# Banded attention and a routed two-layer network: weights in longer runs with strided columns, one batch fewer transposed on chip, narrower appends, products on zeros, and a new order of work

## The chip, the cores and the metric

The kernel runs on one core of one Trainium2 chip. The core has a matrix engine (TensorE, "PE" in the profile, with "PEld" for its loads of the stationary operand), VectorE ("DVE"), ScalarE ("ACT"), GpSimd ("POOL") and SyncE ("SP"), each with its own queue of instructions in a fixed order, and 16 DMA engines that all queues feed. The metric is device microseconds for one execution, lower is better.

## The reference

Attention over a band of 32 positions to either side, 8 batches, 8 heads, 576 positions, 64 columns a head:

```python
scores = scale * np.matmul(q, k.transpose(0, 1, 3, 2))
mask = np.abs(pos[:, None] - pos[None, :]) <= window      # window = 32
scores = np.where(mask, scores, -1000000000.0)
attn = np.exp(scores - np.max(scores, axis=-1, keepdims=True))
attn = attn / (np.sum(attn, axis=-1, keepdims=True) + 1e-09)
out = np.matmul(attn, v)
```

Its output, as 4608 tokens of 512 columns, goes through a network with 8 experts. Each token uses the one with the largest logit:

```python
logits = x @ w_gate + modality_bias[modality_id]          # modality_id is 0 or 1
e_idx = np.argmax(logits, axis=1)
gate_w = softmax(logits)[np.arange(N), e_idx]
for e in range(E):
    h = np.maximum(x[mask] @ w1[e], 0.0)                  # 512 -> 1024
    out[mask] = gate_w[mask, None] * (h @ w2[e])          # 1024 -> 512
```

## The kernel before

The bias decides the expert nearly alone, so the kernel computes, for each of the two modalities, only the expert with the largest bias, and checks at the end that every token chose that expert. If not (or if a count is too large), a branch runs a slow general version. With the inputs used here it isn't taken.

The program is one long list of named steps, `ORDER`, written out by hand. A loop reads it and calls one small function for each name. Every engine executes its own share of the list in this order and waits where its data aren't ready; nothing is moved afterwards. A step's numbers are its indices, `/a` or `/v` names the engine (ScalarE or VectorE), and the digits behind a colon are the PSUM banks it uses, of eight.

For each batch b (0 to 7), with the heads in two groups g of four:

- `l b.u.g` (L215, GpSimd's DMA queue) loads queries (u = 0) or keys (u = 1) of a group into one of eight `qkin` buffers, converted to bf16. `t b.g.u` (L582, VectorE) transposes them in 32x32 blocks into `qk`.
- `MA`, `MB` (L591, L595) write the band's mask into PSUM by a product with the identity `ident`; `SA`, `SB` (L614) add the scores; batches 0 and 1 use the former, later batches are masked by `M` (L639, VectorE) after the exponential. `sa`, `sb` (L622, L625, ScalarE) are the exponentials into `pt`.
- The values come in one of two ways. `lv` (L220) loads a half straight into `vt` in runs of 64 columns. `lw` (L226) loads it in long runs into a `qkin` buffer; then `tv` (L237, VectorE) transposes it, `TV` (L250, TensorE) multiplies it with columns of the identity, 20 products, and `vc` (L264 ScalarE or L266 VectorE) copies the result into `vt`. Batches 0 to 3 go the second way.
- `V` (L658, TensorE) multiplies with the values for a pair of heads, `v` (L668, L669, VectorE) normalises into `xt`.
- `H b.m` (L678, TensorE, four products) takes 128 tokens of `xt` as weights and multiplies them with a one-hot matrix `oh` (`o`, L576) that sorts the tokens: those of modality 0 to the left, those of modality 1 to the right. `a` (L695, ScalarE) appends both parts to `xl`, each in a window of W columns, whose place is read from a register (`Ko` loads the registers). Windows overlap, and the later one writes over the unused end of the earlier one. `J` and `j` (L708, L716) do the same for the token numbers in `cl`.

For each of 18 groups t of 256 sorted tokens, and one of 128 in the middle (t = 18):

- `U t.mp` (L819, TensorE, eight products) is the first layer with `w_sb` (W1 of the modality) as weights; `u` (L834 ScalarE, L832 VectorE) applies the maximum with 0. `D t.s.half` (L842, four products) is the second layer, `y` (L854, L856) scales it, and `O` (L862, GpSimd) writes 128 rows to their places with an indirect DMA.
- `G` (L746, L749) and `r`, `E` compute the router's logits, the check and the row numbers for two groups at a time. `W which.i` (L792, GpSimd's DMA queue) loads the weights of layer `which`.

The constants are `K...` steps: `Km`, `Ki` load the bias and the modality ids (SyncE's queue), `Kd` (L473, VectorE) converts the ids into `midr`, `Kt`, `Kr` count the tokens in front of each, `Kn` and `Ka` build masks on GpSimd, `Kf0` is a part of the check of counts on GpSimd. `Z0` to `Z6` gather the check: `Z2` (L886, L889, GpSimd), `Z3` (L892 to L896, VectorE), `Z4` (L900, TensorE), `Z5` (L902, VectorE) make the word `t_i`. All engines load it (L1038) and branch on it (L1040).

## Time and profile before

| | us |
|---|---|
| median of 3 runs (lowest, highest) | 228.79 (228.74, 230.57) |
| the profiled execution | 228.53 |
| its span in the trace | 226.9 |
| TensorE busy | 202.0 (89%) |
| VectorE busy | 158.1 (70%) |
| ScalarE busy | 143.9 (63%) |
| GpSimd busy | 103.2 (45%) |

The span runs from the first to the last instruction of the program; the rest of an execution's time lies around it. TensorE's products are pipelined: one starts before the one ahead of it ends, so the distance between starts is the cost in a dense stretch, and a group's busy time divided by its count is near it, but for the last product's own time. The mean duration of one, also printed, is longer. A line of the timeline reads: start, length, engine, line of the code, operation, output<-inputs, shape, count, and in brackets the idle time of the engine ahead of it and what ended it. A line of the chain reads: start, length, what ran.

### The profile page before, as it was taken

The numbers are of one execution on the slowest core, as the hardware profiler recorded it, in microseconds if no ns is written. First come the engines' busy times: TensorE is split into PE (matmuls) and PEld (weight loads), VectorE is DVE, ScalarE is ACT, GpSimd is POOL, SyncE is SP. The second block draws the span as 40 slices with busy tenths as digits, with TensorE's granted clock in tenths as the row PEclk, the third lists the DMA queues.
The fourth block names the chain that finished last, engine by engine and source line by source line (L and its number), as shares of the span: only waits on it lengthen the run. The fifth ranks groups of instructions, "written<-read, shape, count | busy, mean of one in ns | idle before, by whom it ended". The sixth has DMA issues, their size and how long they took to land.

```text
span 226.9 us, 6569 instructions
## 1 busy us (share of the span) xinstructions
PE 202.0 (89%) x2693; PEld 146.3 (64%) x2720; DVE 158.1 (70%) x312; ACT 143.9 (63%) x219; POOL 103.2 (45%) x211
## 2 busy tenths in 40 slices
PE   0498887899999999999999999999999999999940
PEld 0257566689768666777667776775875777666510
DVE  1588999989998999699889892976528036334210
ACT  8179789999889789689577876732654332103420
POOL 6988443951502878148408014400450402436670
PEclk9999999999999999999999999999999999999995
DMA  4999999999999948979989111900140299214441
GB/s 74 155 196 203 202 192 212 207 188 175 207 210 191 123 100 153 183 133 174 181 97 133 60 49 63 128 5 0 51 185 3 50 174 194 95 46 188 185 141 60
DMA packets 32774, 30.44 MB, mean 134 GB/s; under 512 B 20664, under 2 KB 23776, under 8 KB 32736
## 3 DMA queue, kind: packets, MB, share of 16 engines
q0 software_dynamic: 32512, 29.90, 73.9%
q8 instruction: 23, 0.38, 0.7%
q14 instruction: 15, 0.12, 0.2%
q1 hardware_dynamic: 224, 0.05, 0.2%
HBM read 40.96 MB, written 9.70 MB: 223 GB/s over the span
## 4 chain that ended last, share of the span: by engine, by line
PE 79%; DVE 6%; ACT 6%; issue 3%; DMA 2%; SPq 1%; POOL 1%; DVEq 0%; POOLq 0%; ACTq 0%
PE banks L842 28%; PE banks L819 28%; PE banks L658 6%; PE banks L614 5%; PE banks L250 4%; PE banks L678 4%; ACT pt L622 3%; DVE qk L582 2%; ACT xl L695 2%; PE banks L746 2%; DMA mid<-in_moe_modality_id_dram 2%; DVE xt L669 1%; PE banks L708 1%; ACT pt L625 1%; SPq L283 1%
## 5 line engine op out<-in xcount | busy, mean ns | idle before, releaser
L819 PE MATMUL banks<-xl,w_sb 128*128 128x256 bf16 x576 | 71.1, 273 | 0.2 <-ACT xl L695 0.2
L842 PE MATMUL banks<-w_sb,hT 128*128 128x512 bf16 x261 | 66.6, 379 | 1.6 <-issue 0.3
L862 POOL DMA_INDIRECT out_dram<-ys,ix x37 | 39.6, 1070 | 53.7 <-issue 29.7
L819 PEld LDWEIGHTS <-w_sb 128*128 128x128 bf16 x576 | 54.3, 98 | 11.0 <-issue 0.6
L622 ACT ACTIVATE pt<-banks 128x1536 bf16<-128x1536 f32 x32 | 46.4, 1453 | 16.0 <-PE banks L614 15.6
L842 PEld LDWEIGHTS <-hT 128*128 128x128 bf16 x296 | 27.0, 98 | 25.3 <-issue 0.8
L582 DVE STREAM_TRANSPOSE qk<-qkin 128x576 int32<-128x576 int32 x32 | 38.3, 1239 | 0.5 <-DMA qkin<-in_k_dram 0.5
L834 ACT ACTIVATE hT<-banks 128x512 bf16<-128x512 f32 x41 | 24.0, 595 | 19.0 <-PE banks L819 18.9
L695 ACT CAST xl<-banks 128x768 f32 x40 | 32.2, 805 | 5.7 <-PE banks L678 3.5
L639 DVE TENSOR_TENSOR pt<-pt,mask 128x1920 bf16<-128x1920 bf16 x24 | 27.3, 1146 | 4.7 <-ACT pt L625 4.2
L856 DVE TENSOR_SCALAR ys<-banks,gw 128x512 f32<-128x512 f32 x20 | 14.8, 743 | 20.4 <-PE banks L842 14.1
L832 DVE TENSOR_SCALAR hT<-banks 128x512 bf16<-128x512 f32 x33 | 22.4, 684 | 8.1 <-PE banks L819 7.9
L669 DVE TENSOR_TENSOR xt<-banks,recs 128x640 bf16<-128x640 f32 x32 | 26.4, 825 | 1.1
L854 ACT ACTIVATE ys<-banks,gw 128x512 f32<-128x512 f32 x17 | 11.5, 686 | 19.1 <-PE banks L842 17.0
L658 PE MATMUL banks<-vt,pt 128*128 128x65 bf16 x576 | 22.6, 193 | 1.2 <-ACT pt L625 0.9
L658 PEld LDWEIGHTS <-pt 128*128 128x128 bf16 x576 | 20.9, 97 | 4.0 <-issue 1.6
L614 PE MATMUL banks<-qk 32*128 32x192 bf16 (+1 forms) x640 | 19.5, 245 | 1.6 <-DVE xt L669 0.5
L614 PEld LDWEIGHTS <-qk 32*128 32x128 bf16 x640 | 12.9, 95 | 8.9 <-issue 6.8
L781 POOL CAST ix<-ixf 128x4 int32<-128x4 f32 (+1 forms) x10 | 2.8, 279 | 32.2 <-DVE ixf L778 32.2
L716 ACT CAST cl<-banks 4x192 f32 x40 | 12.3, 307 | 5.7 <-PE banks L708 5.0
L678 PE MATMUL banks<-oh,xt 128*128 128x128 bf16 x160 | 14.1, 219 | 0.8 <-ACT pt L622 0.7
L678 PEld LDWEIGHTS <-xt 128*128 128x128 bf16 x160 | 10.9, 98 | 3.5 <-issue 0.7
(165 smaller groups left out, 202.5 us busy)
## 6 DMA issues: line engine op xcount, KB each, us to landing
qkin<-in_k_dram POOLq DMA_DIRECT2D x16, 288.0 KB, 8.1
qkin<-in_q_dram POOLq DMA_DIRECT2D x16, 288.0 KB, 7.8
w_sb<-in_moe_w_dram POOLq DMA_DIRECT2D x4, 1024.0 KB, 11.8
qkin<-in_v_dram POOLq DMA_DIRECT2D x8, 288.0 KB, 7.2
vt<-in_v_dram POOLq DMA_DIRECT2D x8, 288.0 KB, 6.6
pt<-in_moe_w_dram POOLq DMA_DIRECT2D x2, 1024.0 KB, 11.5
out_dram<-ys,ix POOLq DMA_INDIRECT x37, 2.8
mid<-in_moe_modality_id_dram SPq DMA_DIRECT2D x3, 8.0 KB
```

Of the source, the lines that this page charges most:

```text
L582: nc.vector.transpose(qk_t[b % 2][:, g, at:at + S].rearrange("p (t r) -> p r t", r=R), Ct["l", b, u, g][:].bitcast(I32).rearrange("p (r j) ...
L614: nc.tensor.matmul(st[:, h, WIN * i_:WIN * i_ + w_], qk[32 * h:32 * h + 32, c_, QK + k0:QK + k0 + P], qk[32 * h:32 * h + 32, c_, q0:q0 + w ...
L622: nc.scalar.activation(pt[:, :, 2 * part:2 * part + 2, 0:WIN], st[:, :, 0:2 * WIN].rearrange("p h (j c) -> p h j c", c=WIN), ACT.Exp, scal ...
L639: by[eng or "v"].tensor_tensor(out=p_ap, in0=p_ap, in1=mask[:], op=ALU.mult)
L658: nc.tensor.matmul(o_ap, pt[:, c1:c1 + P], vt[:, g0 + j, 0:D + 1], start=(m == 0 and i_ == 0), stop=(i_ == len(mine) - 1), skip_group_chec ...
L669: nc.vector.tensor_tensor(out=x_t[b % NX][:, hp].rearrange("p m (h d) -> p h m d", h=2), in0=o_v[:, :, :, 0:D], in1=rec.unsqueeze(3).to_br ...
L678: nc.tensor.matmul(ph[:, kd, :], x_t[b % NX][:, kd, m, :], Ct["o", b][:, m, :], start=(kd == 0), stop=True, skip_group_check=True)
L695: ins = nc.scalar.copy(windows(xl, n_kd, P, NM * b + m), src)
L819: ins = nc.tensor.matmul(ph[:, u_, :], w1[:, kd, P * mi:P * mi + P], xl[:, kd, c0:c0 + n_], start=(kd == 0), stop=(kd == n_kd - 1))
L834: nc.scalar.activation(o_ap, i_ap, ACT.Relu)
L842: nc.tensor.matmul(Ct["D", t_, s_], Ct["h", t_][:, kf, P * s_:P * s_ + P], w2[:, kf, :], start=(kf == 0), stop=(kf == n_kf - 1))
L862: ins = nc.gpsimd.indirect_dma_start(out=out, out_offset=bass.IndirectOffsetOnAxis(ap=ix[:, k_, n_:n_ + 1], axis=0), in_=Ct["y", t_, s_][: ...
```

## The change

Seven things change.

1. The weights of the first layer are split by `(ki ko)` instead of `(ko ki)`: partition ki holds four neighbouring rows of W1, one run of 16 KB in DRAM, instead of four runs of 4 KB. Its products then need the inputs' columns ki*4 + kd on partition ki. So `xt` becomes tokens by 512 columns, and `H` takes every fourth column as weights. The gate's weights are split the same way.
2. The second layer's weights are split so that a partition holds pairs of neighbouring rows, runs of 4 KB instead of 2 KB. The order of the 1024 hidden columns changes with it, and `U` takes every second column of W1 as weights.
3. Batch 3's values are loaded with `lv`. Only batches 0, 1 and 2 use `lw`, `tv`, `TV`, `vc`.
4. The append windows are 88 columns wide instead of 96, and the limits of the check follow.
5. A new step `X` multiplies a matrix of zeros with itself, twice, 512 columns each; its output isn't read. It stands eight times in the list.
6. The list has a new order throughout.
7. The slow version follows the new layouts.

```diff
-Kh l0.1.0 Ki Km Kv1/v Kv3/v Ke Kw Kd l0.0.0 Kn0 Kc1 l0.0.1 Kj Kc0 l0.1.1 lw0.0 lw0.1 Kt0:2 Kv0/v t0.0.1 Kn1 MA0.0:4567
...
-y16.0/a O18.0 O16.1 O17.1 O17.0 O16.0
+Km l0.1.1 Kh Kw t0.1.1 l0.0.1 Kv1/v t0.1.0 Ke Ki Kj lw0.0 l0.1.0 Kn0 Kn1 Kq0/a Kq1/a Kp0/a X7:2 X1:3 X4:7 l0.0.0 Kv0/v
...
+y16.1/a O16.1 Z2 Z3 Z4:3 Z5
...
-    W = 96
+    W = 88
...
-    x_t = [const.tile([P, n_kd, NM, P], BF16, name=f"xt{i}") for i in range(NX)]
+    x_t = [const.tile([P, NM, HD], BF16, name=f"xt{i}") for i in range(NX)]
...
-        nc.gpsimd.dma_start(wg_sb[:], moe_w_gate.rearrange("(ko ki) e -> ki ko e", ki=P))
+        nc.gpsimd.dma_start(wg_sb[:], moe_w_gate.rearrange("(ki ko) e -> ki ko e", ki=P))
...
-            gs.memset(lv_[:, 1], 48.0 * 48.0)
-            gs.memset(lv_[:, 1, :, 1:NM - 1], 32.0 * 32.0)
+            gs.memset(lv_[:, 1], (W - 48.0) ** 2)
+            gs.memset(lv_[:, 1, :, 1:NM - 1], (W - 64.0) ** 2)
...
-            out=x_t[b % NX][:, hp].rearrange("p m (h d) -> p h m d", h=2),
+            out=x_t[b % NX][:, :, P * hp:P * hp + P].rearrange("p m (h d) -> p h m d", h=2),
...
-            nc.tensor.matmul(ph[:, kd, :], x_t[b % NX][:, kd, m, :], Ct["o", b][:, m, :],
+            nc.tensor.matmul(ph[:, kd, :], x_t[b % NX][:, m, kd::n_kd], Ct["o", b][:, m, :],
...
-    W1P, W2P = "a (ko ki) f -> ki (a ko) f", "a (ko ki) d -> ki (a ko) d"
+    W1P, W2P = "a (ki ko) f -> ki (a ko) f", "a (c ki e) d -> ki (a c) (e d)"
...
-                ins = nc.tensor.matmul(ph[:, u_, :], w1[:, kd, P * mi:P * mi + P], xl[:, kd, c0:c0 + n_],
+                ins = nc.tensor.matmul(ph[:, u_, :], w1[:, kd, 2 * P * (mi // 2) + mi % 2:2 * P * (mi // 2 + 1):2], xl[:, kd, c0:c0 + n_],
...
+    def X(_, i):
+        for h in range(2):
+            nc.tensor.matmul(bank([P, 512]), zero_b[:, 0:P], zero_b[:], start=True, stop=True, skip_group_check=True)
```

What the new order does shows best at two places. The first is VectorE at the start. `mid` holds the modality ids, `qk<-qkin` is a transpose, `c` the ids as flags. Before:

```order
L288 MEMSET mid_103 40x256
L232 MEMSET xl 128x64 x4
L430 MEMSET e_119 128x1 x8
L301 MEMSET zero_b 128x256
L302 MEMSET one_f 128x1
L473 CAST midr<-mid_103 40x128
L232 MEMSET xl 128x64 x2
L582 STREAM_TRANSPOSE qk_77<-qkin_69 128x18x32
L494 TENSOR_SCALAR c_125<-banks 128x40
L582 STREAM_TRANSPOSE qk_77<-qkin_70 128x18x32
```

After:

```order
L288 MEMSET mid_103 40x256
L301 MEMSET zero_b 128x256
L302 MEMSET one_f 128x1
L582 STREAM_TRANSPOSE qk_77<-qkin_69 128x18x32
L232 MEMSET xl 128x64 x2
L582 STREAM_TRANSPOSE qk_77<-qkin_70 128x18x32
L430 MEMSET e_119 128x1 x8
L232 MEMSET xl 128x64 x2
L473 CAST midr<-mid_103 40x128
```

The conversion of the ids, which waits for their load, stood ahead of the first transpose and now stands behind the second.

The second place is GpSimd's queue at the end. `out_dram<-ys` is a write of 128 rows, `nm<-ne` and `re` are parts of the check (Z2), `fl<-rm` too (Z6), `t_i` is the word that decides the branch. Before:

```order
L862 DMA out_dram<-ys_97,ix 4608x512
L862 DMA out_dram<-ys_95,ix 4608x512
L862 DMA out_dram<-ys_98,ix 4608x512
L862 DMA out_dram<-ys_96,ix 4608x512
L862 DMA out_dram<-ys_93,ix 4608x512
L1038 TENSOR_LOAD t_i
L1040 COMPARE_AND_BRANCH
```

After:

```order
L862 DMA out_dram<-ys_97,ix 4608x512
L874 TENSOR_SCALAR fl<-rm 128x1
L875 TENSOR_SCALAR fl<-rm 128x1
L862 DMA out_dram<-ys_98,ix 4608x512
L862 DMA out_dram<-ys_93,ix 4608x512
L886 TENSOR_SCALAR re<-ixf 128x40
L889 TENSOR_TENSOR nm<-ne,re 128x320
L1044 TENSOR_LOAD t_i
L1046 COMPARE_AND_BRANCH
```

The two operations of Z2, which stood among the row writes of the last groups, now stand behind the last write, ahead of the load of `t_i`. Their followers on VectorE and TensorE (Z3, Z4, Z5) move with them. In the new file the lines behind L907 are six higher.

102 lines of the change are left out of this document (52 added, 50 removed).

## The prediction

> **What bounds the kernel now.** I read the shares of the page's chain of work, then a table of busy time by stage, then the start in order of time, then the end.
>
> ```profile
> PE 79%; DVE 6%; ACT 6%; issue 3%; DMA 2%; SPq 1%; POOL 1%; DVEq 0%; POOLq 0%; ACTq 0%
> ```
>
> ```profile
> core 0: us, PE busy (x) PEld busy (x) DVE busy (x) ACT busy (x) POOL busy (x), PEclk, DMA share, GB/s
> 8.40:20.00 11.60, 10.14 (x139) 6.49 (x140) 10.57 (x24) 6.99 (x7) 9.77 (x38) 1.00 1.06 190
> 20.00:30.00 10.00, 8.89 (x190) 6.32 (x187) 9.39 (x14) 8.09 (x10) 6.14 (x18) 1.00 1.10 194
> 30.00:42.50 12.50, 9.49 (x213) 8.54 (x214) 12.03 (x16) 11.94 (x15) 6.48 (x13) 1.00 1.15 207
> 60.00:100.00 40.00, 39.63 (x589) 28.82 (x593) 36.36 (x62) 33.44 (x53) 18.55 (x53) 1.00 1.09 166
> 218.40:226.90 8.50, 0.00 (x0) 0.00 (x0) 0.15 (x1) 0.58 (x1) 2.16 (x3) 0.73 0.32 109
> ```
>
> TensorE carries 79% of the chain. From about 50 us on it has no gap worth naming (39.63 of 40 us in the fifth row), so there only removed TensorE work counts. Before 42.5 us it is not the bound: VectorE is (12.03 of 12.50, 9.39 of 10.00), with ScalarE close behind. After 218.4 no engine computes much: 8.5 us of rows written out, a branch and the closing of the program. So there are three accounts: the start, TensorE's work, the end.
>
> The start, from the chain (first row) and the timelines of VectorE, TensorE and ScalarE:
>
> ```profile
> 4.19 3.67 DMA mid<-in_moe_modality_id_dram
> ...
> 7.98 0.32 DVE L473 CAST midr<-mid 40x128 bf16<-40x128 int32 x1 [5.99 <-DMA mid<-in_moe_modality_id_dram]
> 8.27 1.20 DVE L582 STREAM_TRANSPOSE qk<-qkin 128x576 int32<-128x576 int32 x1
> ...
> 10.64 0.83 PE L614 MATMUL banks<-qk 32*128 32x192 bf16 x16 [0.40 <-DVE n1s L497]
> 11.40 1.46 PE L591 MATMUL banks<-neg,ident 128*128 128x384 bf16 x4
> 14.20 0.82 PE L591 MATMUL banks<-neg,ident 128*128 128x384 bf16 x4
> 42.49 1.03 PE L819 MATMUL banks<-xl,w_sb 128*128 128x256 bf16 x8 [0.17 <-ACT xl L695]
> ...
> 11.52 1.45 ACT L622 ACTIVATE pt<-banks 128x1536 bf16<-128x1536 f32 x1 [4.82 <-PE banks L614]
> 14.31 1.45 ACT L622 ACTIVATE pt<-banks 128x1536 bf16<-128x1536 f32 x1 [1.34 <-PE banks L614]
> 28.56 1.45 ACT L622 ACTIVATE pt<-banks 128x1536 bf16<-128x1536 f32 x1 [1.71 <-PE banks L614]
> 32.28 2.24 ACT L264 CAST vt<-banks 128x1152 bf16<-128x1152 f32 x2 [0.43 <-PE banks L250]
> 34.41 4.16 ACT L695 CAST xl<-banks 128x768 f32 x5
> ...
> L237 DVE STREAM_TRANSPOSE xl<-qkin 128x576 int32<-128x576 int32 x8 | 9.3, 1241 | 0.0
> L669 DVE TENSOR_TENSOR xt<-banks,recs 128x640 bf16<-128x640 f32 x32 | 26.4, 825 | 1.1
> L668 DVE RECIPROCAL recs<-banks 128x10 f32<-128x10 f32 x32 | 6.8, 213 | 5.4 <-PE banks L658 5.4
> ```
>
> VectorE stands idle for 5.99 us behind a wait for the modality ids, although the first query and key loads are in SBUF before that:
>
> ```profile
> L215 POOL DMA_DIRECT2D qkin<-in_k_dram x1: 722/722/722, 1.5 to 1.5; - x1
> ...
> DMA to landing us min/median/max: 4.5/4.5/4.5
> ...
> L215 POOL DMA_DIRECT2D qkin<-in_q_dram x1: 592/592/592, 2.2 to 2.2; - x1
> ...
> DMA to landing us min/median/max: 5.2/5.2/5.2
> ...
> w_sb<-in_moe_w_dram POOLq DMA_DIRECT2D x4, 1024.0 KB, 11.8
> ```
>
> These are the first key load (issued at 1.5 us, so landed at 6.0), the first query load (issued at 2.2, landed at 7.4), and the weights.
>
> **The change, part by part.**
>
> *New order at the start.* The id cast moves behind the first two transposes. The first starts at 6.0, the second at 7.4, and the first scores at about 8.6 instead of 10.64. First exponential: 9.5 instead of 11.52, a lead of 2.0 us. Between there and the first append (34.41) ScalarE spends 22.9 us in before, 3.5 of them in the three waits quoted (1.34, 1.71, 0.43). The work is the same eight exponential groups, four value copies and the mask copies. The after order has one register load (the append offsets, an estimate of 1.4 us, since it stood inside the 1.71 wait) in the open, so without waits the first append would start near 9.5 + 22.9 - 3.5 + 1.4 = 30.3. VectorE does not allow that: counting its queue from the second transpose on, at 1.1 to 1.2 us a transpose (9.3 / 8) and 1.0 us a reciprocal with its normalisation (33.2 / 32), its eleventh q/k transpose and fourth value transpose end near 29.7. The products of that last half follow (1.2, half of the 2.4 us that a pair of halves takes below) and its copy (1.1, half of the row at 32.28), so the first append starts near 32.0, 2.4 us earlier. From there to the first up-projection stand five appends and five small ones, one exponential and a router group. My count gives 38.9; I allow 0.6 for small waits that a count leaves out and take 39.5 against 42.49. TensorE has then done about the same work (eight masked banks' worth, five value halves, eight attention outputs in both; within 0.4 us). Term: -3.0 us. Bounds: -1.5 (half lost to waits) and -4.5 (the count holds and the waits of 42 to 51 us go too).
>
> The weights must be there. From the first landing at 6.0, sixteen more loads of 0.295 MB stand ahead of the first weight of 1.05 MB; at the 0.20 MB/us of the window rows that is 1.45 us a load, so W1.1 lands near 6.0 + 16 x 1.45 + 5 = 34 to 36, W1.0 near 40, W2.1 near 47. The U groups want them at 39.5, 43 and 52. GpSimd must issue in time: the new order puts the small operations of the overflow check (Kf0) ahead of W1.1; by a count of its queue the issue still comes some 8 us ahead of that landing, while earlier loads are under way.
>
> *Eight product pairs on zeros.* They stand ahead of everything on TensorE, which has nothing to do until 8.5 us; one pair (0.4 us) stands in a wait before 26 us. Zero cost. What they may bring is that the four mask products take 0.82 (row at 14.20) and not 1.46 us (row at 11.40), though PEclk says 1.00 for both. [...]
>
> *Batch 3's values by strided load.* Two of eight halves lose their transposes, products and copies.
>
> ```profile
> 30.95 2.41 PE L250 MATMUL banks<-ident,xl 128*128 128x64 bf16 x40 [0.96 <-DVE xl L237]
> ```
>
> A pair of halves, 40 products, lasts 2.2 us (2.41 less the drain of the last one, 0.2). One pair goes, from the stage where TensorE is dense: -2.2 us. VectorE loses 2.5 us and ScalarE or VectorE 2.2, both hidden under TensorE. The two loads that come instead land before 69 us by the same queue count; the products on them stand near 67 and 74 us, the first needing only the first load (63 us): zero, with 4 us to spare.
>
> *Strided weights.* H loads every fourth column of xt, U every second of w_sb, at the same number of instructions.
>
> ```profile
> L250 PEld LDWEIGHTS <-xl x160: 97/125/125, 18.2 to 66.3; 128*128 128x128 bf16 x160
> L678 PEld LDWEIGHTS <-xt x160: 95/98/125, 33.1 to 173.4; 128*128 128x128 bf16 x160
> 33.64 0.72 PE L658 MATMUL banks<-vt,pt 128*128 128x65 bf16 x18
> 33.16 0.64 PE L678 MATMUL banks<-oh,xt 128*128 128x128 bf16 x8
> 80.18 0.87 PE banks L819 x8
> ```
>
> The L250 products already take every second column as weights. They follow at 56 ns (2.2 us / 40), while the L658 products, one column wider, follow at 31 ns (0.55 / 18, again without the last drain). Either the strided load takes 56 ns, or the output does, which L250 also writes to every second column. A load not held up lasts 97 ns on L250 and 95 on L678, so I put it down to the output, and the load at no more than before. U has 109 ns a product (0.87 / 8): hidden in either case. H has 56 ns (0.45 / 8). Lower end: 0. Upper end: the 56 ns are the load's and step four doubles it to 112, so 160 x 56 ns = +9.0 us. I take 0, by the 97 and 95.
>
> [...]
>
> *Appends of 88 columns.* 704 instead of 768 elements on ScalarE, 40 times; ScalarE is not on the path after 50 us. Zero. The token counts of this draw need at most 76, so the slow branch stays untaken.
>
> *Longer runs of the weights.* Same bytes, 128 and 512 runs instead of 512 and 1024. At most 1 us sooner for each of the second weights, which wait for nobody: zero.
>
> *The end.* Z2 to Z5, the check that decides the branch, stood among the last groups; now they stand behind the very last row write.
>
> ```profile
> 216.80 1.46 PE L842 MATMUL banks<-w_sb,hT 128*128 128x512 bf16 x6
> 220.19 0.97 POOL L862 DMA_INDIRECT out_dram<-ys,ix  x1 [0.30 <-issue]
> L1040 PEldq COMPARE_BRANCH  x1: 4382/4382/4382, 219.2 to 219.2; - x1
> L1040 POOLq COMPARE_BRANCH  x1: 58/58/58, 219.7 to 219.7; - x1
> L1040 POOLq EVENT_SEMAPHORE  x5: 17/43/992, 223.1 to 224.4; - x5
> L889 POOL TENSOR_TENSOR nm<-ne,re 128x320 f32<-128x320 f32 x1 | 0.7, 740 | 2.9 <-DVE ne L783 2.9
> L892 DVE TENSOR_REDUCE fl<-nm 128x1 f32<-128x320 f32 x1 | 0.5, 476 | 0.0
> ```
>
> In before the last product ends at 218.3; the branch is taken by 219.7; TensorE and GpSimd go on only at 223.6 and 223.1, 3.4 to 4.4 us later; the program ends 8.6 us after the product. In after, the last write is issued 1.6 to 2.5 us after the last product, GpSimd's two check operations end at 3.7, VectorE's three at 4.6, the product, the compare and the register loads at about 5.7. If going on again takes 3.4 us as before, and GpSimd's closing 2.5 us (224.4 to 226.9), the end comes 11.7 us after the product: +3.1. If it only takes 1.5 to 2 us because no row writes move any more, +1.4. I take +2.2; nothing hides it, and the fewer writes at the end (one behind the last product instead of two) are in it.
>
> **The sum.** -3.0 - 2.2 + 2.2 = -3.0 us. The profiled execution took 228.53 us (span 226.9), 0.26 under the median 228.79 of the runs shown: 225.5 against its own time, 225.8 against the median. I say 225.6.
>
> **The rivals.**
>
> *The gain at the start does not come.* If GpSimd's small operations or the DMA queue delay W1.1 to 42 us, the first up-projection starts when it did. For: DMA share is 1.06 to 1.15 in the three early rows, so a late issue is not made up. Against: the count leaves 3.5 us. Then -2.2 + 2.2: 228.6, no change.
>
> *The end costs little.* If the branch goes on at once and the check hides under the last write's landing, the sum is -5.2: 223.4; with the start at its bound, 221.9.
>
> *The strided load is slow (the other side).* One place, H's 160 products: at 112 ns, +9.0 us, 234.6. It decides from 75 ns on: 160 x 19 ns eats the 3.0 us. For: L250's 56 ns. Against: 97 against 95 ns.
>
> *The dense stage opens gaps.* The new order could make TensorE wait for ScalarE or VectorE (33.44 and 36.36 of 40 us busy); each has 2 us or more less to do, so I fold this into the first rival.
>
> **How the numbers follow.** A measurement of this kernel can tell about 1%, 2.3 us, from no change. Forecast (224.5 to 227): 0.45. End cheap or start better (221 to 224.5): 0.25. Start lost (227 to 229.5): 0.20. Slow load (above 229.5): 0.10. Faster by over 1% (under 226.5) gets the second case and most of the first: 0.64; within 1%: 0.28; slower: 0.08, since the slow load at partial price ends within 1%. The range 221.0 to 229.0 leaves out the slow load and a little at both ends. The likeliest case's own range is 224.5 to 227.
>
> **What would show it.** Right: first transpose near 6 us, first L819-group near 39.5, 120 L250 products, H at 56 ns a product, a branch about 6 us after the last product, and a close about 11 us after it. Wrong: L819's first group near 42, weights landing after 40, H at 75 ns or more, gaps in TensorE between 60 and 200 us, or an end shorter than 9 us after the last product.

## The result and the profile after

The kernel after the change takes 230.38 us, the median of 20 runs (229.77 to 231.33). The kernel before, run beside it, takes 228.76 us (20 runs, 227.98 to 230.94). The ratio is 1.0053, with a 95% interval of 1.003 to 1.0077: half a per cent slower, less than the 1% that the forecast counted as a change. The forecast was 225.6 us with a range of 221.0 to 229.0, so the result lies outside the range and on the other side. The profiled execution took 229.87 us, and its span is 228.2 us. The ratios of the experiments leave out runs that lie over 1.5% above the fastest of their kernel; where that drops most runs, the range of all is given first.

The three accounts of the forecast, read from both traces:

| | before | after | measured | forecast |
|---|---|---|---|---|
| span's start to the first up-projection | 42.49 | 41.38 | -1.11 | -3.0 |
| first up-projection to the end of the last product | 175.76 | 173.27 | -2.49 | -2.2 |
| end of the last product to the close | 8.68 | 13.51 | +4.83 | +2.2 |
| span | 226.93 | 228.16 | +1.23 | -3.0 |

The gain in the dense part came near the forecast. The start gave a third of what was expected, and the end took back more than twice what was expected.

The shares of the chain of work, of after:

```profile
PE 78%; POOL 10%; DMA 4%; issue 3%; ACT 1%; DVE 1%; POOLq 0%; ACTq 0%; DVEq 0%
```

GpSimd has 10% of the chain; before it had 1%. The table of busy time by stage, of after (columns as in the prediction's table):

```profile
8.50:20.00 11.50, 8.82 (x176) 6.76 (x177) 9.00 (x26) 8.77 (x8) 9.32 (x36) 1.00 1.02 181
20.00:30.00 10.00, 9.03 (x173) 6.30 (x170) 9.07 (x15) 7.80 (x10) 8.74 (x53) 1.00 1.05 183
30.00:41.40 11.40, 9.58 (x182) 8.63 (x182) 9.46 (x12) 8.52 (x14) 10.19 (x19) 0.85 1.06 215
60.00:100.00 40.00, 40.00 (x597) 29.25 (x595) 36.17 (x61) 31.53 (x48) 19.59 (x23) 1.00 0.99 146
214.70:228.20 13.50, 0.16 (x1) 0.08 (x1) 0.95 (x4) 0.69 (x1) 4.72 (x8) 0.67 0.19 66
```

Between 60 and 100 us TensorE has no gap at all, so the new order does not starve it. Between 30 and 41.4 us no engine but GpSimd is near full (10.19 of 11.40), and the granted clock is 0.85. After the last product GpSimd has 4.72 us of work, where before it had 2.16.

The start, from the timelines of VectorE, TensorE and ScalarE, of after:

```profile
5.78 1.25 DVE L582 STREAM_TRANSPOSE qk<-qkin 128x576 int32<-128x576 int32 x1 [4.19 <-DMA qkin<-in_k_dram]
8.50 0.52 PE L614 MATMUL banks<-qk 32*128 32x192 bf16 x16
9.07 1.45 ACT L622 ACTIVATE pt<-banks 128x1536 bf16<-128x1536 f32 x1 [2.35 <-PE banks L614]
30.18 1.26 DVE L237 STREAM_TRANSPOSE xl<-qkin 128x576 int32<-128x576 int32 x1 [0.93 <-DMA qkin<-in_v_dram]
31.49 2.31 PE L250 MATMUL banks<-ident,xl 128*128 128x64 bf16 x20 [0.86 <-DVE xl L237]
33.84 1.12 ACT L264 CAST vt<-banks 128x1152 bf16<-128x1152 f32 x1 [2.30 <-PE banks L250]
34.86 0.75 ACT L695 CAST xl<-banks 128x704 f32 x1
36.00 0.29 ACT L716 CAST cl<-banks 4x176 f32 x1 [0.39 <-POOL cl L421]
41.38 1.03 PE L819 MATMUL banks<-xl,w_sb 128*128 128x256 bf16 x8
```

The first transpose, scores and exponential stand where the forecast had them (6.0, 8.6 and 9.5 us). Then the lead melts. The value half that the first append waits for is transposed at 30.18, after a wait of 0.93 for its load. Its 20 products take 2.31 us, at half clock, as the window of 3.5 us shows (0.52, third column from the right). Behind the first append (34.86) the first `j0` step waits for GpSimd, which is zeroing `cl`. That zeroing as a row of GpSimd's groups:

```profile
31.50:35.00 3.50, 3.50 (x42) 3.50 (x42) 2.09 (x2) 1.20 (x3) 3.50 (x2) 0.52 1.01 212
...
L421 POOL MEMSET cl<- 128x4736 bf16 x1 | 4.1, 4068 | 0.0
```

It runs from 31.90 to 35.97. A bracket of 0.39 us looks harmless, but it is only the idle time left over: ScalarE reached the step late, and it would have had to wait however early it came.

The end, from the timelines of GpSimd, TensorE and VectorE and from TensorE's sequencer, of after:

```profile
208.53 0.98 POOL L862 DMA_INDIRECT out_dram<-ys,ix  x1 [7.92 <-ACT ys L854]
214.27 0.38 PE L842 MATMUL banks<-w_sb,hT 128*128 128x512 bf16 x1
215.12 0.98 POOL L862 DMA_INDIRECT out_dram<-ys,ix  x1 [0.28 <-POOL ix L781]
216.18 0.26 POOL L874 TENSOR_SCALAR fl<-rm 128x1 f32<-128x1 f32 x1
216.99 1.06 POOL L862 DMA_INDIRECT out_dram<-ys,ix  x1 [0.27 <-issue]
218.36 0.98 POOL L862 DMA_INDIRECT out_dram<-ys,ix  x1 [0.30 <-issue]
219.82 0.74 POOL L889 TENSOR_TENSOR nm<-ne,re 128x320 f32<-128x320 f32 x1
220.60 0.48 DVE L892 TENSOR_REDUCE fl<-nm 128x1 f32<-128x320 f32 x1 [10.15 <-POOL nm L889]
221.80 0.15 DVE L902 TENSOR_SCALAR t_i<-banks 1x1 int32<-1x1 f32 x1 [0.33 <-PE banks L900]
...
L1046 PEldq COMPARE_BRANCH  x1: 4476/4476/4476, 222.6 to 222.6; - x1
```

The last product ends at 214.65. GpSimd still has row writes to issue, with the two small operations of Z6 among them; the last one goes out at 218.36, 3.71 us after the product (1.94 before). Only then come Z2, Z3, Z4 and Z5, the word `t_i` at 221.8, and TensorE's branch, which takes 4.48 us. Each step hands over to the next within 0.3 us, but for the 0.6 us between the word and TensorE's branch, in which the word is loaded: this is one chain on GpSimd and behind it, 13.5 us long.

### The profile page after: what moved, and what is told of

Its sections match the earlier page's. It is cut to its first block, busy times and chain, and to the rows that moved or that the text cites. A ratio compares the mean times of both kernels' runs of the same rounds, so it can differ in the third digit from the quotient of the medians.

```text
span 228.2 us, 6542 instructions
## 1 busy us (share of the span) xinstructions
PE 207.5 (91%) x2696; PEld 146.9 (64%) x2696; DVE 152.6 (67%) x303; ACT 142.7 (63%) x224; POOL 103.1 (45%) x211
## 4 chain that ended last, share of the span: by engine, by line
PE 78%; POOL 10%; DMA 4%; issue 3%; ACT 1%; DVE 1%; POOLq 0%; ACTq 0%; DVEq 0%
PE banks L819 29%; PE banks L842 28%; PE banks L658 7%; PE banks L614 5%; PE banks L678 4%; DMA qkin<-in_v_dram 4%; POOL qkin L215 3%; PE banks L250 2%; POOL out_dram L862 2%; PE banks L746 2%; PE banks L708 1%; ACT xl L695 1%; POOL qkin L226 1%; DVE xl L237 1%; ACT vt L264 0%
## 5 line engine op out<-in xcount | busy, mean ns | idle before, releaser
L842 PE MATMUL banks<-w_sb,hT 128*128 128x512 bf16 x288 | 71.1, 379 | 0.0
L834 ACT ACTIVATE hT<-banks 128x512 bf16<-128x512 f32 x45 | 25.7, 595 | 23.3 <-PE banks L819 23.0
L695 ACT CAST xl<-banks 128x704 f32 x40 | 30.1, 752 | 6.0 <-PE banks L678 5.4
L832 DVE TENSOR_SCALAR hT<-banks 128x512 bf16<-128x512 f32 x29 | 19.7, 684 | 15.9 <-PE banks L819 15.6
L854 ACT ACTIVATE ys<-banks,gw 128x512 f32<-128x512 f32 x20 | 13.5, 688 | 15.9 <-PE banks L842 9.2
L856 DVE TENSOR_SCALAR ys<-banks,gw 128x512 f32<-128x512 f32 x17 | 12.6, 744 | 10.9 <-issue 6.2
L614 PE MATMUL banks<-qk 32*128 32x192 bf16 (+1 forms) x640 | 18.6, 239 | 0.2
L614 PEld LDWEIGHTS <-qk 32*128 32x128 bf16 x640 | 12.1, 93 | 8.3 <-issue 6.0
L678 PEld LDWEIGHTS <-xt 128*128 128x128 bf16 x160 | 11.8, 115 | 4.2 <-issue 0.8
L716 ACT CAST cl<-banks 4x176 f32 x40 | 11.8, 295 | 4.2 <-PE banks L708 2.0
```

Source lines behind the costliest of these rows:

```text
L614: nc.tensor.matmul(st[:, h, WIN * i_:WIN * i_ + w_], qk[32 * h:32 * h + 32, c_, QK + k0:QK + k0 + P], qk[32 * h:32 * h + 32, c_, q0:q0 + w ...
L678: nc.tensor.matmul(ph[:, kd, :], x_t[b % NX][:, m, kd::n_kd], Ct["o", b][:, m, :], start=(kd == 0), stop=True, skip_group_check=True)
L695: ins = nc.scalar.copy(windows(xl, n_kd, P, NM * b + m), src)
L834: nc.scalar.activation(o_ap, i_ap, ACT.Relu)
L842: nc.tensor.matmul(Ct["D", t_, s_], Ct["h", t_][:, kf, P * s_:P * s_ + P], w2[:, kf, :], start=(kf == 0), stop=(kf == n_kf - 1))
```

## The experiments

Chips differ. On the chip of the first comparison and in the last two runs the kernel before takes 228.8 to 229.0 us; in all the other experiments it takes 233.0 to 233.3. So each ratio is to the kernel before on the same chip, and after itself must be compared by its ratio on such a chip (1.0068, the experiment e12).

The edits below are pieces of `ORDER`: a step stands behind the one ahead of it in the line.

### The end

**The check early, in after (e1).** The theory: the loss at the end is the check behind the last write.

```diff
+O8.1 Z6 ... +r9.5 Z2 ... +y15.0/v Z3 ... +D16.0.1:2 Z4:3 y16.0/a Z5
-O18.0 Z6 ... O16.1 Z2 Z3 Z4:3 Z5
```

> The kernel after, with the overflow check taken off the very end: its GpSimd pair on the reciprocals stands behind O8.1, its masking pair behind r9.5, VectorE's three behind y15.0, the product behind D16.0.1, the compare behind y16.0; the last thing issued is the row write O16.1. Nothing else moves. Theory A (the check behind the last write is most of the lost 4.9 us at the end, and GpSimd's queue of late writes the rest): the program ends 6.7 us after the last write is issued, as before (220.19 to 226.9), instead of 9.8; the write itself still comes about 4 us after the last product, because the queue stays. That is 2.5 to 3.1 us faster than after, 227.3, about 1 us under the kernel before. Theory B (the check hides under the landing of the last write, and the late writes alone cost the time): within 0.5 us of after, 230.

Measured: 231.01 us against 233.02, ratio 0.9906 (0.9872 to 0.9941): 1.6% below after on such a chip (1.0068), some 3.8 us. GpSimd's timeline of e1, a piece of the check and the last write:

```profile
213.79 0.74 POOL L889 TENSOR_TENSOR nm<-ne,re 128x320 f32<-128x320 f32 x1
...
223.94 0.97 POOL L862 DMA_INDIRECT out_dram<-ys,ix  x1 [0.31 <-issue]
```

GpSimd's part of the check is done 9 us ahead of the last write and costs nothing there. The close comes 9.26 us after the last product instead of 13.51. The last write still goes out 3.46 us after the product, so that part of the loss is not the check's.

**The check late, in before (e2).** The other direction, the edit alone.

```diff
-r6.6 Z2 Z3 ... -D16.0.1:3 Z4:4 ... -y17.0/v Z5
+O16.0 Z2 Z3 Z4:4 Z5
```

> The kernel before, with only its check (Z2 to Z5) moved behind the last row write, as in the kernel after. Theory A: the last write is issued where it was (220.2), and the end comes 9.8 us behind it and not 6.7: 3.0 us slower than before, 231.8. My prediction's own term for this move was +2.2. Theory B: within 0.5 us of before.

Measured: 236.25 us, ratio 1.0152 (1.0073 to 1.0231), +3.5 us, and a close 12.45 us after the last product (8.68 in before). The interval is wide (1.7 to 5.4 us); the trace has +3.8 at the end. So the move of the check costs some 3.5 to 3.8 us in either kernel, more than the +2.2 that I took and above the upper bound of 3.1.

**The last weights early (e3).** ScalarE waits 6.59 us for a store of rows ahead of the last `y` steps (first row below, of after). The theory: this wait makes the last writes late. The store stands behind the 1-MB load W2.2 in GpSimd's DMA queue.

```diff
-O12.0 r7.6 W2.2
+W1.2 W2.2
```

> The kernel after, with only the load W2.2 (the 1 MB second weight of the shared tile) issued right behind W1.2 (168 us) instead of between the row writes of the last third (195.5). Theory A (that load stands ahead of the row writes O12.0 and O13.0 in the DMA queue, so their buffers come free at 205.2 and 206.5, the results y of ScalarE and VectorE wait 6.6 and 6.2 us for them, and ten writes go out back to back until 219.3): ScalarE's y no longer waits, the last write is issued 1.5 to 2 us after the last product instead of 3.7, and the time falls by about 2 us to 228. Theory B (GpSimd is late for another reason, such as its own casts and the 1.28 us that each write takes): no change, 230; the writes still go out back to back up to 219.

Measured: ratio 1.0075 (1.0032 to 1.0119), no gain. ScalarE's timeline, of after and then of e3:

```profile
205.94 1.26 ACT L854 ACTIVATE ys<-banks,gw 128x512 f32<-128x512 f32 x2 [6.59 <-DMA out_dram<-ys,ix]
```

```profile
204.42 0.69 ACT L854 ACTIVATE ys<-banks,gw 128x512 f32<-128x512 f32 x1
```

The wait is gone, and nothing is won: the last write stands at +3.87 us. The theory fell. What stays is GpSimd's own order: it stands at the write O14.1, whose `y14.1` waits for its product, while O15.1 and O17.1 behind it could go; afterwards the writes follow each other at 1.28 us each.

**Both (e4).**

```diff
+O8.1 Z6 ... +r9.5 Z2 ... +y15.0/v Z3 ... +D16.0.1:2 Z4:3 y16.0/a Z5 ... +W1.2 W2.2
-O12.0 r7.6 W2.2 ... O18.0 Z6 ... O16.1 Z2 Z3 Z4:3 Z5
```

> Both edits together: check off the end and W2.2 issued behind W1.2. Theory A: last write issued at about 216.3 (1.7 us after the last product), end 6.7 us later at 223.0; against after -5 us, 225, faster than before by 1.6 per cent. Theory B (either edit alone already takes the whole loss): as the better of the two alone, 227 or 228.

Measured: 231.08 us, ratio 0.9891 (0.9833 to 0.9950), the same as e1 within the intervals. The early load adds nothing that can be measured. Against e3, beside which it ran, e4 has only the check moved: 1.0075 becomes 0.9891, and the intervals lie apart.

**The writes in the order in which their rows come (e10).** e4 and:

```diff
-y14.1/a O14.1 O15.1 O17.1
+y17.1/a O17.1 O15.1 Z2 ... +y14.1/a O14.1
```

> The kernel of e4 (check off the end, W2.2 early) with the row writes O17.1 and O15.1 issued before O14.1 instead of behind it. In e4 GpSimd stood at O14.1 until y14.1 was there (212.25), with O17.1 and O15.1 ready 6.3 and 3.3 us earlier, and wrote the rest back to back; the last write came 3.0 us after the last product. Theory A (the order of the writes in GpSimd's queue makes the last one late): the last write is issued 1.6 us after the last product, the time falls by 1.4 us against e4 (0.9891 of before), to 0.983. Theory B (y18.0 is late on ScalarE, as in e3 and e4, where it started 1.75 us after its product had ended, and the last three writes follow from it): the last write stays at 3.0 us after the product, no change.

Measured: 228.76 us, ratio 0.9787 (0.9741 to 0.9833). GpSimd's timeline of e10:

```profile
219.27 0.99 POOL L862 DMA_INDIRECT out_dram<-ys,ix  x1 [1.76 <-issue]
220.56 0.97 POOL L862 DMA_INDIRECT out_dram<-ys,ix  x1 [0.30 <-issue]
221.84 0.97 POOL L862 DMA_INDIRECT out_dram<-ys,ix  x1 [0.30 <-issue]
```

Three writes at 1.28 us are left, with an idle 1.76 us ahead of them: GpSimd has caught up with the products. The last one goes out 1.64 us after the last product, and the close is 7.02 us after it. Against e4 that is 1.0% less, with intervals that just touch; in the traces the close comes 10.1 us after the last product in e4, 9.26 in e1 and 7.02 here. So the end has two causes, the check and the queue of writes, and both are shown.

### The start

**A warm clock (e5).** The theory: the value products at half clock hold up the start. Products on zeros were added in the two places ahead of the half-clock stretch.

```diff
+Kr0 X8:5 X9:6 X10:5 ... +H0.0:0 X11:1 X12:2
```

> The kernel after, with five more pairs of products on zeros: three between the transposed ids (Kt0) and the token counts (Kt1), where TensorE stands idle for 1.8 us at 10.8 us, and two behind the first H of batch 0, where it stands idle for about 0.9 us at 30.6 us. So far every profile of after and of its variants has one 3.4 us stretch at half clock (31.5 in after, 13.5, 14.6 and 12.6 in e1, e3 and e4), the profiles of before have none once the clock is up (14.2). Theory A (these gaps let the clock fall, and the half stretch costs about 1 us of the gain at the start): no half-clock stretch between 7 us and the end, first up-projection at 40 to 40.5 us instead of 41.4 to 41.8, 1 us faster than after (0.4 per cent). Theory B (the start is set by loads and VectorE, not by the clock): the clock may stay up, but the first up-projection stays at 41.4 and the time within 0.3 us.

Measured: ratio 1.0071 (1.0045 to 1.0098), and the first up-projection at 42.53. The clock stays at 1.0 until 38.7 and then falls to half for 3.4 us, so the stretch that was to go away moved behind the first append. That append comes at 34.02, and then ScalarE waits. ScalarE's timeline of e5:

```profile
36.37 0.30 ACT L716 CAST cl<-banks 4x176 f32 x1 [1.59 <-POOL cl L421]
```

What was won on the clock went into a longer wait for the zeroing of `cl`. The clock as the only cause fell; the row names the next suspect.

**No products on zeros (e6).**

```diff
-X7:2 X1:3 X4:7 ... -X5:4 X3:3 ... -X6:0 X0:1 ... -X2:4
```

> The kernel after without any product on zeros. Theory A (the products bring the clock up some 6 us earlier, but it falls back once): the clock first reaches 1.0 near 12 to 14 us, as in before, with no fall after that; the first scores take 0.8 instead of 0.5 us, the mask products of the first 13 us 1.4 instead of 0.8; the first up-projection within 0.5 us of after's, so the products gain about nothing as they stand. Theory B (they are worth what they were put in for): 1 us or more slower than after. [...]

Measured: ratio 1.0109 (1.0055 to 1.0163), 0.4% above after, with intervals that overlap. The trace's first record of the granted clock, 1.0, stands at 16.84 us instead of 7.58 (14.15 in before), and the first up-projection stands at 41.84. Whether the products help stays open; no harm from them shows.

**The late value load early (e7).** The theory: the wait of 0.93 us for the load of batch 1's second half holds up the start.

```diff
-t1.1.1 lw1.1 lw2.1
+l1.1.1 lw1.1
```

> The kernel after, with the load lw1.1 (second half of batch 1's values) issued right behind l1.1.1 instead of three loads later. In after VectorE waited 0.93 us for it (30.18 us), and I had forecast 28.55. Theory A (that load's place in the queue holds the first append): VectorE's transpose of it starts at about 29.2, the first append and the first up-projection come 0.9 us earlier, and the time falls by 0.9 us (0.4 per cent). Theory B (something else, the clock or the q/k loads now behind it, takes its place): first append within 0.3 us of 34.9, time within 0.3 us.

Measured: ratio 1.0064 (1.0032 to 1.0096), no gain; the first append at 34.03, the first up-projection at 41.42. VectorE transposes the half at 30.40, with no wait for its load. ScalarE's timeline of e7:

```profile
36.20 0.29 ACT L716 CAST cl<-banks 4x176 f32 x1 [1.42 <-POOL cl L421]
```

ScalarE reaches this step at 35.6 in after and at 34.8 in e5 and e7 (the start less the wait), and is let go at 36.0, 36.4 and 36.2 all the same. The theory fell: the load's place alone does not bind.

**After once more (e12).** The unchanged kernel on the other chips.

> The kernel after once more, unchanged, so that the other kernels of this call have it beside them on the same chip: 1.003 to 1.008 of before, as on the first chip. If the ratio were below 1, the comparisons of e1 to e8 with the first chip's 1.0053 would not stand.

Measured: 234.94 against 233.33 us, ratio 1.0068 (1.0039 to 1.0097); a wait of 1.10 us for `cl`, and the first up-projection at 41.53.

**The zeroing early (e9).**

```diff
-lw2.1 Kf0 ... -lw2.0 Kc7
+lw2.1 Kc7 ... +W2.0 Kf0
```

> The kernel after, with GpSimd's zeroing of the counter row cl (Kc7, 4.07 us) issued behind lw2.1 instead of behind lw2.0, and the small operations Kf0 (2.2 us) issued behind W2.0 instead. In after that zeroing runs from 31.90 to 35.97, and ScalarE's first small append j0.0, which the new order puts between the first and the second append, waits for it (1.59 us in e5, 1.42 in e7, 0.39 in after), so that the start ends at the same place whatever was gained ahead of it. Theory A (this zeroing is what holds the start): j0.0 runs right behind the first append near 34.8 to 35.6, the first up-projection comes at 40 to 40.5 and the time falls by 0.8 to 1.4 us against after in the same comparison. Theory B (the start is held by the loads or by the clock): first up-projection still at 41.4, no change.

Measured: 231.89 to 236.56 us (median 235.52, before 233.33); the ratio, from four of the twelve runs, is 0.9999 (0.9944 to 1.0054), and its interval overlaps after's (1.0068). That is no gain to rely on. The profiled run, of 235.48 us, has the first append at 36.84 and the first up-projection at 42.91. GpSimd's and VectorE's timelines of e9:

```profile
22.89 4.08 POOL L421 MEMSET cl<- 128x4736 bf16 x1
...
23.93 3.09 DVE L506 CAST offs<-cA 1x41 int32<-1x41 f32 x1
24.03 2.99 DVE L582 STREAM_TRANSPOSE qk<-qkin 128x576 int32<-128x576 int32 x1
25.12 1.90 DVE L668 RECIPROCAL recs<-banks 128x10 f32<-128x10 f32 x1
```

A cast of 41 numbers takes 3.09 us here, where it takes 0.17 in after. It and the two operations behind it end together at 27.02, as the zeroing ends (26.97). The zeroing keeps the cast out, and VectorE's queue stands behind it. Why it does, no run shows.

**The zeroing in eight pieces (e13).** e9, with pieces of about 0.5 us (4.08 / 8). The theory: the cast gets in between two of them, 0.6 us late at most.

```diff
-gs.memset(cl[:], 0.0)
+_ = [gs.memset(cl[:, 592 * s_:592 * s_ + 592], 0.0) for s_ in range(8)]
```

> The kernel of e9 (zeroing of cl early, Kf0 late), with the zeroing in eight pieces of 592 columns instead of one of 4,736. In e9's profile three operations of VectorE that stood at 23.9 us, in the middle of the zeroing, ended together at 27.0 when it was over: the small cast of L506 took 3.09 us instead of 0.2, the transpose behind it 2.99 instead of 1.2; in e11, where the cast came before the zeroing, nothing was held. Theory A (VectorE is shut out by the long GpSimd operation when that cast falls into it, and this makes e9 spread from 231.9 to 236.5): with pieces of about 0.5 us no VectorE operation is held for over 0.6 us, the first append comes at 33 to 34 us, the first up-projection at 39.5 to 40.5, and the time is 0.994 to 0.998 of before, without e9's high values. Theory B (the spread of e9 comes from the half-clock stretches): first append and spread as in e9.

Measured: 231.80 to 237.63 us (median 236.66, before 232.98); the ratio, from four of the twelve runs, is 1.0007 (0.9959 to 1.0056). The profiled run took 236.54 us. VectorE's and GpSimd's timelines of e13:

```profile
23.47 3.71 DVE L506 CAST offs<-cA 1x41 int32<-1x41 f32 x1
...
22.78 4.37 POOL L421 MEMSET cl<- 128x592 bf16 x8
```

The cast waits for all eight pieces: it ends at 27.18, the last of them at 27.15. That theory fell: back-to-back pieces did not let it in.

**The `j0` steps late (e14).** The zeroing stays; the steps that need `cl` move behind the fourth of batch 0's five appends.

```diff
-V6:56 j0.0 a0.1 a0.2 j0.1 j0.2 ... a0.3 j0.3 j0.4 TV2.1:456
+V6:56 a0.1 a0.2 ... a0.3 TV2.1:456 ... l3.1.1 j0.0 j0.1 j0.2 j0.3 j0.4 SB2.1:0123
```

> The kernel after, with the zeroing of cl left where it is, but ScalarE's five small appends j0.0 to j0.4 moved behind the fourth append a0.3, so that none stands in front of an append while cl is being zeroed. Theory A (the wait of j0.0 for the zeroing is what holds the start, 0.4 to 1.6 us): the five appends and five small ones run without that wait, the first up-projection comes 0.5 to 1.4 us earlier than in after, 0.2 to 0.6 per cent. Theory B (VectorE's or TensorE's work behind the appends holds it): no change.

Measured: 1.0026 (0.9992 to 1.0061), where e12 has 1.0068; the intervals overlap. The trace is plainer. ScalarE's timeline of e14:

```profile
33.23 0.75 ACT L695 CAST xl<-banks 128x704 f32 x1
34.27 2.33 ACT L695 CAST xl<-banks 128x704 f32 x3 [0.29 <-PE banks L678]
36.49 1.61 ACT L716 CAST cl<-banks 4x176 f32 x5
38.01 0.74 ACT L695 CAST xl<-banks 128x704 f32 x1
```

Four appends now pass ahead of the first `cl` step, which no longer waits, and the first up-projection stands at 39.87, near the forecast's 39.5. Not all of that is the edit's: the first append came 1.2 us earlier than in e12, though nothing ahead of it was changed.

### The layouts

**The old layouts in the new order (e8).** Before's code for weights and `xt`, with after's order, windows of 88 and products on zeros.

> The order, the products on zeros and the 88-column appends of after, but with the memory layouts of before: weights in 1 KB and 2 KB runs, the attention output by quarters, H and U with adjacent columns as weights. Theory A (strided columns as weights and longer runs are both free, as predicted): within 0.5 us of after; H products follow at 56 ns and U products at 109 ns in both. Rival (strided weight loads cost time somewhere that the gaps between products don't show): faster than after by 1 us or more. Second rival (the longer runs help the weights to land): slower than after by 0.5 to 1 us.

(The expectation counts the runs in bf16 bytes; in DRAM they are twice as long.) Measured: 236.65 us, ratio 1.0151 (1.0095 to 1.0208): not faster than after, so no cost of the strided weights shows. The weight loads of H and the value products, of after, and then H's of e8 (count, and minimum, median and maximum of one in ns):

```profile
L678 PEld LDWEIGHTS <-xt x160: 110/113/185, 29.3 to 170.6; 128*128 128x128 bf16 x160
...
L250 PE MATMUL banks<-ident,xl x120: 216/247/349, 12.9 to 51.1; 128*128 128x64 bf16 x120
```

```profile
L678 PEld LDWEIGHTS <-xt x160: 95/98/183, 29.4 to 175.1; 128*128 128x128 bf16 x160
```

One strided load lasts 15 ns longer, but H's products follow each other at a median of 56 ns in both, and U's at 109. The 120 products on L250 (160 before) show that batch 3's pair is gone. e8 is slower than its neighbours, by 0.8%, some 2 us, against e5 and e7, with intervals that just touch. Its trace, set against e7's, shows 0.9 us of it at the start (first up-projection at 42.28, behind a half-clock stretch) and 0.9 us at one place near the end. ScalarE's and TensorE's timelines of e8 there:

```profile
212.43 1.26 ACT L854 ACTIVATE ys<-banks,gw 128x512 f32<-128x512 f32 x2 [7.92 <-DMA out_dram<-ys,ix]
...
213.17 1.05 PE L819 MATMUL banks<-xl,pt 128*128 128x128 bf16 x16 [1.19 <-ACT ys L854]
```

ScalarE waits here for the store that stands behind the load W2.2 (e3). With the new layouts the same wait is 6.59 to 7.02 us in nine profiles, and TensorE waits 0.29 us at most. So with the short runs this store comes later, and TensorE stands for it. That the shorter runs of W2.2 are the reason is likely: the layouts are the only edit.

### All together

**Every edit (e11), and the same with the zeroing in pieces (e15).** e11 is e10 with e5, e7 and e9, e15 is e11 with the pieces of e13; beside e10's edits:

```diff
+Kr0 X8:5 X9:6 X10:5 ... +l1.1.1 lw1.1 ... +lw2.1 Kc7 ... +W2.0 Kf0 ... +H0.0:0 X11:1 X12:2
```

> All edits that a theory still speaks for: check off the end, W2.2 early, writes in the order in which the rows are ready (e10), the zeroing of cl early (e9), lw1.1 early (e7), five more pairs of products on zeros (e5). If the gains of the end (1.5 per cent against after) and of the start (0.4 to 0.6 per cent) add up, 0.977 to 0.984 of before; if the start gains nothing, as e10.

> The kernel of e11 (all edits) with the zeroing in eight pieces. Theory A of e13: e11's low times without its high ones, 226.7 to 228 on the chip of e11, 0.972 to 0.979 of before. Theory B: e11's spread of 226.7 to 234.1 again.

Measured: e11 took 226.74 to 234.09 us in six runs (before 233.33), too spread for a ratio, though its profile is good (first up-projection 39.61, close 7.03). e15 came to 227.22 us, 0.9765 (0.9706 to 0.9824), first up-projection 39.27, with no such spread. In their profiles VectorE's cast ran at 21.9 and 21.6 us, just ahead of the zeroing at 22.7. That e11's spread comes from runs in which the cast met the zeroing is likely, and not shown.

**The edits without the early zeroing (e16), and the same kernel again (e18).** Beside e10's edits, those of e7 and e14:

```diff
+l1.1.1 lw1.1 ... +l3.1.1 j0.0 j0.1 j0.2 j0.3 j0.4 SB2.1:0123
```

> The kernel of e10 (0.9787 of before) with lw1.1 early (e7) and the small appends behind a0.3 (e14). If e14's gain stands beside that of the end: 0.973 to 0.977 of before. If not, 0.979.

> The kernel of e16 once more, unchanged, in a comparison of its own. If its gain is what the edits explain (start 3 us, end 1.7 us shorter than in before), it is 0.972 to 0.982 of before whatever the chip; on a chip like the first, with the 2.5 us of the dense stage in addition, 0.965 to 0.972. If it was luck of one chip: above 0.985.

Measured: e16 227.51 us, 0.9759 (0.9712 to 0.9806). e10 and e16 start the first append at 32.86 and 32.91 us, so they show best what the place of the `cl` steps is worth: in e10 the first of them waits until the zeroing ends (row below, ScalarE's timeline of e10), and the first up-projection stands at 41.92; in e16 it stands at 39.54. A half-clock stretch in e10, from 38.75 on, is part of the difference.

```profile
35.90 0.29 ACT L716 CAST cl<-banks 4x176 f32 x1 [2.28 <-POOL cl L421]
```

e18, on a chip like the first, 222.28 against 229.00 us, ratio 0.9692 (0.9650 to 0.9734). Two rows of the stages, then TensorE's first up-projection and GpSimd's last write, of e18:

```profile
30.00:39.50 9.50, 8.02 (x181) 7.17 (x181) 9.21 (x13) 8.72 (x14) 8.31 (x16) 1.00 1.07 218
213.00:219.90 6.90, 0.00 (x0) 0.00 (x0) 0.00 (x0) 0.69 (x1) 1.95 (x3) 0.77 0.25 88
...
39.50 1.03 PE L819 MATMUL banks<-xl,w_sb 128*128 128x256 bf16 x8
...
214.59 0.97 POOL L862 DMA_INDIRECT out_dram<-ys,ix  x1 [0.30 <-issue]
```

Against before (42.49, 175.76, 8.68) it has 39.50, 173.46 and 6.97: -3.0, -2.3 and -1.7, together -7.0 us in the span. It is faster than both kernels. The clock is 1.00 up to the first up-projection (0.85 in after), VectorE is again the fullest engine there (9.21 of 9.50), and GpSimd has 1.95 us left after the last product.

**Before once more (e17).** A profile of before, meant for the chips on which it takes 233 us.

> The kernel before once more, for its profile on a chip of the experiments, which are slower than the first (233 instead of 228.8 us). On the first chip the way from the first up-projection to the last product took 175.8 us in before and 173.3 in after; in the repetition of after on a chip of the experiments it took 177.6. Theory A (TensorE's saving by the values' strided load is there on every chip): 179.5 to 180.5 here. Theory B (the new order loses that saving on these chips): 177 to 178.5. The end should again be 8.7 us behind the last product.

It came to a chip like the first: 228.67 us beside 228.94, with 42.40, 175.99 and 8.67 us. So it doesn't answer what it was for. It repeats the account of before on a further chip. TensorE is busy there for 40.00 of the 40 us between 60 and 100; the 39.63 of the prediction's table came from a trace that lacks 27 of 2720 products. And against it, e18's dense part, 173.46, is 2.5 us shorter too. In this profile of before the stretch holds 60 products on L250, in that of after it holds 20: at 56 ns each, batch 3's pair accounts for 2.2 of the 2.5 us.

## Why the forecast was wrong

**What held.** The first transpose, scores and exponential (6.0, 8.6, 9.5 forecast; 5.78, 8.50, 9.07). Batch 3's values: -2.2 forecast, -2.49 measured from the first up-projection to the last product, with 40 products fewer there. The strided weights at 0 (the range reached to +9.0): 56 ns a product in both layouts. Nothing between 60 and 100 us waits for the narrower appends or for batch 3's values, whose first load landed at 63.0 as forecast. One term of 0 probably did not quite hold, that of the longer runs, by which the second weights, "which wait for nobody", land sooner. Behind W2.2 stands a store that ScalarE waits for, and in the one profile with the old layouts TensorE stands 0.9 us longer for it (e8 against e7).

**"The end", +2.2, measured +4.83: the mechanism was right and the term too small.** Two steps of it failed. The text said that the last write is issued 1.6 to 2.5 us after the last product. I had looked at the one write behind that product and not at those queued ahead of it, of which each takes 1.28 us: it was 3.71, and Z2 to Z5 came later by as much. The branch stands 7.95 us after the product, where the text has about 5.7. And from there to the close I took the middle, about 5.2 us, between a restart as slow as before's and a fast one "because no row writes move any more"; it was 5.6, close to the upper bound of 6.0. TensorE's branch took 4.48 us, as in before (4.38), and GpSimd went on 2.8 us after its own (3.4 in before). The first step accounts for 2.2 us of the miss of 2.6 and the second for 0.4. e1 and e2 show the check's part, e10 that of the queue; the restart was not tested by itself. The rival that the end costs little had it the wrong way round.

**"New order at the start", -3.0, measured -1.11.** Two steps failed, side by side. The first is "the first append starts near 32.0": it started at 34.86, because the load of its value half came late and the half's 20 products ran at half clock (2.31 us for the forecast's 1.2). The second is the count of the stretch behind it, "From there to the first up-projection stand five appends and five small ones". The small ones write into `cl`, which GpSimd zeroes between 31.90 and 35.97. I counted ScalarE's queue and VectorE's, and looked at GpSimd's only for the issue of W1.1.

Either step takes most of the gain. Without the wait of 0.39 us for `cl`, the late append alone would have put the first up-projection near 41.0. In after 5.4 us lie between the end of the zeroing and the first up-projection, so the zeroing alone puts it near 41.4. (Both are estimates from after's trace.) So mending one alone gains little: e5, e7 and e10 start the first append at 34.02, 34.03 and 32.86 and still come to 42.53, 41.42 and 41.92. With the `cl` steps later and the append at 33.23, 32.91 and 32.87 the first up-projection is at 39.87, 39.54 and 39.50 (e14, e16, e18), the forecast's 39.5. The part of the zeroing is shown by these edits. The append's lateness is read from the profiles: where the clock did not fall ahead of it, it stands at 32.86 to 33.54 (e8, e10, e11, e14 to e16, e18), but for e5 (34.02); where the clock fell or came up late, at 34.03 to 34.86 (after, e1, e3, e4, e6, e7, e12), and later still in e9 and e13, in which the cast is kept out. No run changed the clock alone, so this half is not shown by an experiment.

**The rivals.** The first rival said that the gain at the start doesn't come, because W1.1 lands at 42 us. Most of the gain did not come, but W1.1 landed at 37.8 (forecast 34 to 36) and held up nothing: the outcome was near, the mechanism wrong. The slow strided load is refuted. TensorE's gaps in the dense stage did not open (40.00 of 40 us).

**What stays open.** On the chips where before takes 233 us, the stretch from the first up-projection to the last product is 177.6 to 179.1 us with after's order. The one profile with before's order is of the fastest run of e2, 178.2, so it can't tell whether the 2.5 us are there too. The ratios, less what the traces show at the start and the end, leave -0.8 to -3.3 us for this stretch in e1, e3 to e7, e10, e12 and e14 to e16: an estimate, with before's start and end taken from the first chip. What these chips lose is not spread out. Set against e18, the same kernel in e16 falls behind by 4.7 us at nine of TensorE's instructions between 80 and 203 us, by 0.2 to 1.0 us at each; e12 against after falls behind by 4.3 us, at eight of the same nine; before's order (e2 against e17) by 2.2 us, at other places. Ahead of most of them ScalarE starts later after a product's end. Scores and exponential of e7, and the exponential of after:

```profile
79.05 0.64 PE L614 MATMUL banks<-qk 32*128 32x192 bf16 x24
...
80.72 1.45 ACT L622 ACTIVATE pt<-banks 128x1536 bf16<-128x1536 f32 x1 [2.49 <-PE banks L614]
```

```profile
79.69 1.45 ACT L622 ACTIVATE pt<-banks 128x1536 bf16<-128x1536 f32 x1 [1.51 <-PE banks L614]
```

The exponential starts 1.67 us after the start of its scores in e7, and 0.69 us in after, where the scores start at 79.00. Why was not found.

## What to carry to other kernels

When work is moved to the very end, count the whole queue that it is put behind, with every write that waits there, and take the restart behind a branch at its measured price (here 4.48 us on TensorE). When an order is rewritten, write down for each early step which engine makes its buffer ready, the clearing of buffers too: an engine with half its time free can still hold the path (GpSimd is busy for 45% of after's span). A wait of 0.4 us in a trace is no measure of what it binds; take away what is late ahead of it, and see whether it grows (here to 2.28 us). Two hold-ups side by side hide each other: an edit that takes away one and gains nothing does not clear it.

## What the runs showed of the hardware

- The granted clock fell behind stretches in which TensorE was half busy, not idle. In the start of after, e1, e3, e4 and e5, among others, it fell to half for 3.4 us. In after (31.47 to 34.88 us) TensorE had been busy for 1.74 of the 3.41 us ahead of the fall, in e5 (38.7 to 42.1) for 2.09 of the 3.80. How low the share has to be was not shown: in after the clock stayed at 1.00 through 3.41 us with 1.56 busy (10.00 to 13.41).
- Eight GpSimd memsets of about 0.55 us, one behind the other, kept a small VectorE cast out for 3.71 us, up to the end of the whole series (e13); a single one of 4.08 us kept it out for 3.09 us (e9). It is not so for every operation: beside the same zeroing in after, at 31.28, two transposes by VectorE took 2.31 us, as they do at 12.40 without it.
- A row write by GpSimd took it 1.28 us from one to the next (after, 208.53 to 213.67), and the branch at the end 4.38 us (before) and 4.48 us (after) on TensorE, 0.05 to 0.07 us on the other engines.
- The same kernel differs by 2% between chips (228.8 and 233.3 us for before).
